# First phase of a gated attention and FFN kernel: x tiles and GELU results move on GpSimd's DMA queue instead of SP's

## The chip, the cores and the metric

The kernel runs on one core of one Trainium2 chip. The metric is the device time of one execution in microseconds, as the median over runs. The core has five instruction streams: PE (TensorE, matmuls), DVE (VectorE), ACT (ScalarE), POOL (GpSimd) and SP (SyncE, which here only issues DMAs). Each stream runs in order, and streams wait for each other through semaphores. SP and POOL both issue DMAs. Those of SP are counted as queue q1 in the profile, those of POOL as q0.

## What is computed

The input x has 2048 tokens of width 1024 in bfloat16. Two branches are mixed by a sigmoid gate `g` of `x . gate_w`:

```
for s in range(64):                      # segments of 32 tokens
    h = concat(mem, x[32*s : 32*s+32])   # 8 memory rows and 32 tokens
    q, k, v = h@Wq, h@Wk, h@Wv           # 32 heads of 128
    p = softmax(mask(q k^T / sqrt(128))) # the last mask is causal on 40 rows
    o = (p v) @ Wo
    mem, a[s] = o[:8], o[8:]             # the memory of the next segment
b   = (gelu(x @ w_gate) * (x @ w_up)) @ w_down   # width 3584
out = g * a + (1 - g) * b
```

The recurrence through `mem` makes the 64 segments sequential. The FFN branch `b` doesn't depend on it.

## The kernel before, in words

All instructions are recorded by one helper, `op` (line 79), as (engine, function, what it reads, what it writes). The recorder finds the dependencies between the operations and turns them into semaphore waits. The order on each engine is the order of recording. A DMA also names a `lane`, which is a semaphore of its own; a DMA waits for the one before it on the same lane to land.

**First phase** (lines 402 to 587, some 97 us). It prepares x, computes a part of the FFN and fills the on-chip weight slots.

- `load_x(T)` (472) loads tile T of 128 tokens (256 KB) into one of four buffers `px`. `do_x(T)` (476) transposes it on PE (L485), copies it on ACT into `xTp` (L489, L490) and its last columns on DVE into `xr` (L491). POOL multiplies it by `gate_w` into the single buffer `gp` (L493) and DVE reduces that into `dl` (L498). So a `px` buffer has two readers, PE and POOL.
- After four tiles, `xTp` and `xr` are stored to HBM as `xq_scr` (L500) and `xr_scr` (L503). There are two buffers of each.
- `pre_j(fb, j)` (451) computes one of the first four of 28 FFN feature blocks for one of four blocks of 512 tokens: two groups of eight matmuls (L446) and `gelu` (432: L434, L437 on ACT; L435, L438, L440 on DVE) into `gpre[fb % 2]`. When four are done, `gpre` is stored to HBM as `g_scr[fb]` (L458). The FFN loads it at the end of the kernel.
- `more` and `more_late` issue weight pieces (`fetch`, L370) of 512 KB into slots `sl`, three pieces a step.

The loop (566 to 583) walks 16 steps (fb, j). In each it records the next `do_x`, the loading of the tile four further on, three weight pieces, the stores that are due, and `pre_j`. All these DMAs are recorded on SP. The stores wait in two lists, `puts` and `slow`:

```python
now, puts[:], slow[:] = list(puts), slow, []
```

A store in `puts` is recorded in the next step. A store in `slow`, which is the one of `gpre`, passes into `puts` first and is recorded one step later.

**Recurrent loop** (lines 859 to 1006). A segment's 64 weight pieces are walked in an order called `ORDER` (k0, q0, v0, k1, q1, o0, v1, o1; 0 and 1 are halves of the heads). Projections are L758 and L770. The last 8 tokens of each segment, the tails, don't depend on the memory row by row, so their q, k and v are computed for four segments at a time (`fill`, L785) and pass through HBM: `qk_scr` (L831, all on one lane `fq`) and `v_scr` (L826). POOL issues these stores and loads them again, the value tails into `vB` by `load_v` (L522). In segment 0, the tails of the first groups are made and stored between the projections, and `load_v(0, ...)` is called once for each half of the heads: the first recorded at v0, step 4, together with `rest_k(0)`, the second at k1. `attend_tail` (L734) reads `vB`. Some weight slots are shared by two pieces, and the second is fetched when the first is used up, such as six of the `Wv` pieces in segment 0. Every segment ends with the copy of the new memory into `hT` (L994).

**Second FFN part** (lines 1050 to 1107): the other 24 feature blocks, the down projection (L1098) and the mix into `out`.

Of the kernel before, what the change touches and what calls it, by code (L numbers as in the profile page):

```python
# [30 lines left out]
class _Prog:  # L31
# [47 lines left out]
    def op(self, eng, fn, rd=(), wr=(), lane=None, after=()):  # L79
        o = _Op(eng, fn)  # L80
        if lane is not None:
            ln = self.lanes.get(lane)
            if ln is None:
                ln = self.lanes[lane] = [self.new_sem(f"{self.name}_{lane}"), 0, None]
            if ln[2] is not None:
                o.deps.append(ln[2])
            ln[1] += 16
            o.sem, o.val, o.inc, o.need = ln[0], ln[1], 16, True
            ln[2] = o
        for r in rd:  # L90
            self._touch(o, r, False, lane is not None)
        for r in wr:
            self._touch(o, r, True, lane is not None)
        o.deps.extend(after)
        if eng == "pool" and lane is None:
            if self.pool is not None:
                o.deps.append(self.pool)
            self.pool = o
        for d in o.deps:
            d.need = True  # L100
        o.idx = len(self.ops)
        self.ops.append(o)
        return o
# [92 lines left out]
def bass_gated_mix__memory_aug_recurrent_mem_tr__geglu_ffn__prompt_kernel(  # L196
# [15 lines left out]
    xf = A_x.flatten_outer_dims()  # L212
# [18 lines left out]
    with ExitStack() as es:  # L231
# [21 lines left out]
        g_scr = nc.dram_tensor("g_scr", [NFB, 128, NJP * FB], BF16)  # L253
# [91 lines left out]
        op = P.op  # L345
# [45 lines left out]
        for g in range(4):  # L391
            q = slice(32 * g, 32 * g + 32)
# [13 lines left out]
        NPX = min(NT, 4)  # L406
        px = [al(f"px{i}", [128, D]) for i in range(NPX)]
# [43 lines left out]
        def pre_j(fb, j):  # L451
            bg, bu = 2 * (j % 2), 2 * (j % 2) + 1
            for bk, w in ((bg, wgp), (bu, wup)):
                up(w[2 * j // NJP], xTp[fb % 2], bk, 128 * (j % (NJP // 2)))
            g = gpre[fb % 2]
            gelu(PB[bg][:, 0:FB], PB[bu][:, 0:FB], bg, bu, j, g[:, j, :], g.r(j * FB, (j + 1) * FB))
            if j == NJP - 1:
                slow.append(lambda: op("sp", lambda e: e.dma_start(g_scr[fb], g[:, :, :].rearrange("p j c -> p (j c)")), rd=[g.r()],  # L458
                                       wr=[("D", "g", fb)], lane=f"gw{fb % 2}"))

        puts, slow = [], []
# [7 lines left out]
                ins = e.transpose(PBV[5][:, kc * 8:(kc + 1) * 8], pm[0:8, kc * 128:(kc + 1) * 128], ident[0:8, 0:8])  # L469
            return ins  # L470

        def load_x(T):
            if T < NT:
                op("sp", lambda e: e.dma_start(px[T % NPX][:, :], xf[T * 128:(T + 1) * 128, :]), wr=[px[T % NPX].r()], lane=f"px{T % NPX}")

        def do_x(T):
            t = px[T % NPX]
# [43 lines left out]
        def load_v(s, us=slice(0, 2)):  # L521
            op("pool", lambda e: e.dma_start(vB[:, us, :].rearrange("p u c -> p (u c)"),  # L522
                                             v_scr[s][:, :, us, :].rearrange("i h u c -> h i (u c)")),
               rd=[("D", "v", s // 4, g, u) for g in range(4) for u in range(us.start, us.stop)], wr=[vB.r()], lane="vb")

        op("sp", lambda e: e.dma_start(pm[0:8, :], mem0[:, :]), wr=[pm.r()], lane="pm")
        load_x(0)
        op("act", lambda e: e.dma_start(gwb[:, :], gate_w.rearrange("(o d) -> o d", o=1).to_broadcast([128, D])),
           wr=[gwb.r()], lane="gw")
        for T in range(1, NPX):  # L530
            load_x(T)
        def load_pre(h):
            for w, W, nme in ((wgp[h], B_w_gate, "gp"), (wup[h], B_w_up, "up")):
                c0, c1 = h * NJP * 64, (h + 1) * NJP * 64
# [20 lines left out]
        for T in range(TB):  # L555
            do_x(T)
            load_x(T + NPX)
            if T == 0:
                op("dve", lambda e: e.tensor_copy(hT[:, :, NR:32], memT[:, :].rearrange("p (k c) -> p k c", k=KC)),
                   rd=[memT.r()], wr=[hT.r()])  # L560
                op("dve", lambda e: e.tensor_copy(hT[:, :, 0:NR], xTp[0][:, 0, 0, :, 0:NR]),
                   rd=[xTp[0].r(0, KC * SEG)], wr=[hT.r()])
# [3 lines left out]
        for fb in range(NFB):  # L566
            for j in range(NJP):
                T = TB * (fb + 1) + j
                now, puts[:], slow[:] = list(puts), slow, []
                if T < NT:  # L570
                    do_x(T)
                    load_x(T + NPX)
                if T == NT:
                    op("act", lambda e: e.activation(gal[:, :], dl[:, :], ACTF.Exp, scale=-1.0), rd=[dl.r()], wr=[gal.r()])
                    op("dve", lambda e: e.tensor_scalar(out=dl[:, :], in0=gal[:, :], scalar1=1.0, scalar2=None, op0=ALU.add),
                       rd=[gal.r()], wr=[dl.r()])
                    op("dve", lambda e: e.reciprocal(gal[:, :], dl[:, :]), rd=[dl.r()], wr=[gal.r()])
                more(3)
                if T >= NT:
                    more_late(2 if j < 3 and not inits else 0)  # L580
                for f in now:
                    f()
                pre_j(fb, j)
# [250 lines left out]
        def mm0(m, u, b, t, G=0, h=hR):  # L834
            for f in fill(m, u, b, h):
                f()
            act_copy(t[:, :], PB[b][:, :], [BK(b)], [t.r()])
            if m == "v":
                fill_store(m, u, G, t)

        def tr0(m, u, t, n, G=0):
            op("pe", lambda e: trans4(e, t), rd=[t.r(), ident.r()], wr=[BK(TT)])
            fill_put(st0[n], "dve")
            if G == 0:
                x = 256 * u + 128 * (m == "k")
                op("pool", lambda e: e.tensor_copy(qkr[:, u, 0 if m == "q" else 1, :], st0[n][:, 0:128]), rd=[st0[n].r(0, 128)],
                   wr=[qkr.r(x, x + 128)])
            fill_store(m, u, G, st0[n])

        def rest_k(r):  # L850
            op("pool", lambda e: e.tensor_copy(kT[:, :, :, 32:40].rearrange("p j g c -> p (j g) c"),
                                               qkr[:, r, 1, :].rearrange("p (x c) -> p x c", c=8)),
               rd=[qkr.r(256 * r + 128, 256 * r + 256)], wr=[kT.r()])
# [5 lines left out]
        for s in range(NSEG):  # L859
# [12 lines left out]
            def on(m, r, n, *fs):  # L872
                at.setdefault(base_of[m, r] + n, []).extend(fs)
# [10 lines left out]
            if s == 0:  # L884
                on("k", 0, 0, lambda: mm0("v", 0, F1, st0[3]))
                on("k", 0, 0, lambda: mm0("k", 0, F2, tokB))
                if NG > 1:
                    on("k", 0, 0, lambda: mm0("k", 0, F1, tok, 1, hR1))
                    on("k", 0, 4, lambda: tr0("k", 0, tok, 1, 1))
                on("k", 0, 0, lambda: tr0("k", 0, tokB, 0))  # L890
                on("q", 0, 0, lambda: mm0("q", 0, F1, tokB))
                if NG > 1:
                    def q_next():
                        for f in fill("q", 0, F2, hR1):
                            f()
                        tr0("q", 0, tokB, 2)
                        act_copy(tokB[:, :], PB[F2][:, :], [BK(F2)], [tokB.r()])
                    on("q", 0, 0, q_next)
                    on("q", 0, 3, lambda: tr0("q", 0, tokB, 3, 1))
                else:  # L900
                    on("q", 0, 3, lambda: tr0("q", 0, tokB, 2))
                on("v", 0, 4, lambda: (rest_k(0), load_v(0, slice(0, 1))))

                def fills_1():
                    mm0("k", 1, F1, tok)
                    for f in fill("q", 1, F2):
                        f()
                    tr0("k", 1, tok, 1)
                    act_copy(tok[:, :], PB[F2][:, :], [BK(F2)], [tok.r()])
                    mm0("v", 1, F1, st0[2])  # L910
                    tr0("q", 1, tok, 3)
                on("k", 1, 0, fills_1)
                if NG > 1:
                    on("k", 1, 0, lambda: op("dve", lambda e: e.tensor_copy(hR[:, :, :], hR1[:, :, :]), rd=[hR1.r()], wr=[hR.r()]))
                on("k", 1, 0, lambda: (load_v(0, slice(1, 2)), more_late(99)))
                on("q", 1, 0, lambda: load_h(1))
# [73 lines left out]
            if not last:  # L990
                for t, bk in enumerate((B1, B2)):
                    op("pe", lambda e, t=t, bk=bk: e.transpose(PBV[bk][:, 0:128], a_bf[:, 128 * t:128 * t + 128], ident[:, :]),
                       rd=[a_bf.r(128 * t, 128 * t + 128), ident.r()], wr=[BK(bk)])
# [3 lines left out]
                       rd=[BK(bk)], wr=[h_next.r(32 * kc, 32 * kc + 32) for kc in range(t, KC, 2)])  # L997
# [53 lines left out]
        for fb in range(NFB):  # L1051
# [20 lines left out]
            for ps in range(NPS):  # L1072
# [15 lines left out]
                for c in range(NWD):  # L1088
# [3 lines left out]
                    for jj in range(WD):  # L1092
                        j = c * WD + jj

                        def f(e, w=w, jj=jj, j=j, bank=bank, tbs=tbs):
                            for k, tb in enumerate(tbs):
                                for hf in range(2):
                                    ins = e.matmul(PB[bank[2 * k + hf]][:, :], lhsT=GT[:, j, tb * 128:(tb + 1) * 128],  # L1098
                                                   rhs=w[:, jj, hf * 512:(hf + 1) * 512], start=(j == 0), stop=(j == NJ - 1))
                            return ins  # L1100
# [43 lines left out]
```

## Time and profile before

| | us |
|---|---|
| median of 7 runs (lowest to highest) | 2233.7 (2230.86 to 2240.97) |
| the profiled execution's own time | 2235.38 |
| its span, first to last instruction | 2233.6 |
| PE busy | 2083.4 (93%) |
| DVE, ACT, POOL busy | 904.5, 610.7, 616.7 |
| DMA moved | 529.04 MB, mean 237 GB/s |
| first L785 (end of the first phase) | 97.07 |
| first `hT` copy of L994 (end of segment 0) | 151.8 |
| 62 segments from there, mean | 24.49 |

Times in the profile count from the first instruction of the span. A wait line reads "who waited, for whom: total us, times, longest". In the chain of waits each line is a start, a length and what the end of the kernel was waiting for at that time. A name such as `px<-in_A_x_dram` is a DMA by destination and source, with buffer numbers left out.

### The profile page before, as it was taken

The page shows a single profiled execution, that of the slowest core. Times are in us where ns is not written, and L with a number is a line of the kernel's source. Part 1 is how long each engine was busy: PE and PEld are TensorE (multiplying, and loading weights), DVE is VectorE, ACT ScalarE, POOL GpSimd, SP SyncE. Part 2 cuts the span into 40 slices and gives each one's busy share as a digit, 9 for nine tenths or more (in the row PEclk, how much of TensorE's full clock was granted, in tenths as well). Part 3 has the DMA queues.
Part 4 walks back from the last instruction along what each step waited for, and adds up shares of the span by engine and source line. Part 5 has one row for each costly group of instructions (what it writes and reads, how often), then busy time and mean ns, then how long its engine had stood idle before and what let it go on. Part 6 is the DMA issues. An engine that isn't in the chain of part 4 may idle for free.

```text
span 2233.6 us, 80061 instructions
## 1 busy us (share of the span) xinstructions
PE 2083.4 (93%) x36642; PEld 1097.9 (49%) x36642; DVE 904.5 (40%) x2152; ACT 610.7 (27%) x1296; POOL 616.7 (28%) x1139
## 2 busy tenths in 40 slices
PE   7888999999999999999999999999888999999999
PEld 3344555455555545555555545555454444444444
DVE  5433343334334333433433344334434616354362
ACT  4322232323223232323223232223222303122130
POOL 5123333332433343233333423343331000000000
PEclk9889999999999999999999999999999999999999
DMA  9977888788788888887888788778879410001000
GB/s 320 384 266 280 279 308 282 274 301 315 264 290 309 283 275 279 291 291 272 294 298 278 266 296 305 271 272 319 281 268 369 172 38 29 29 24 33 19 29 19
DMA packets 203440, 529.04 MB, mean 237 GB/s; under 512 B 29592, under 2 KB 46616, under 8 KB 203104
## 3 DMA queue, kind: packets, MB, share of 16 engines
q1 hardware_dynamic: 174064, 471.93, 59.2%
q0 software_dynamic: 28896, 51.75, 7.3%
q8 instruction: 287, 4.70, 0.8%
q10 hardware_dynamic: 144, 0.26, 0.1%
q14 instruction: 49, 0.40, 0.0%
HBM read 490.16 MB, written 33.55 MB: 234 GB/s over the span
## 4 chain that ended last, share of the span: by engine, by line
PE 75%; DMA 12%; POOL 5%; issue 4%; DVE 2%; ACT 1%; SPq 1%; DVEq 0%; POOLq 0%
PE pb L758 24%; PE pb L446 16%; PE pb L770 8%; PE pb L1098 8%; PE pb L785 7%; DMA sl<-in_A_Wo_dram 4%; PE pb L670 4%; PE pb L800 3%; DMA a_scr<-a_bf 2%; DMA sl<-in_A_Wv_dram 2%; PE pb L691 2%; DMA sl<-in_A_Wk_dram 1%; POOL v_scr L826 1%; PE pb L685 1%; PE pb L1080 1%
## 5 line engine op out<-in xcount | busy, mean ns | idle before, releaser
L758 PE MATMUL pb<-sl,hT 128*32 128x512 bf16 x12288 | 750.0, 382 | 21.1 <-issue 8.2
L758 PEld LDWEIGHTS pb<-sl,hT 128*32 128x32 bf16 x12288 | 330.8, 97 | 289.8 <-issue 20.5
L770 PE MATMUL pb<-sl,oT 128*32 128x256 bf16 x8192 | 283.5, 277 | 47.7 <-issue 39.9
L658 ACT ACTIVATE tok<-pb 128x512 bf16<-128x512 f32 x317 | 189.3, 597 | 402.1 <-PE pb L758 366.7
L743 POOL COPY oRc<-oT 128x128 bf16<-128x128 bf16 x128 | 97.2, 760 | 639.9 <-DVE oT L661 620.7
L770 PEld LDWEIGHTS pb<-sl,oT 128*32 128x32 bf16 x8192 | 209.7, 97 | 97.9 <-issue 51.2
L785 PE MATMUL pb<-sl,hR 128*32 128x512 bf16 x3072 | 225.5, 384 | 5.9 <-DMA sl<-in_A_Wv_dram 4.9
L446 PE MATMUL pb<-xT,wg 128*128 128x512 bf16 x768 | 183.1, 382 | 4.1 <-DMA wg<-in_B_w_gate_dram 4.1
L446 PE MATMUL pb<-xT,wu 128*128 128x512 bf16 x768 | 181.7, 379 | 0.0
L1098 PE MATMUL pb<-wd,GT 128*128 128x512 bf16 x784 | 169.9, 379 | 0.0
L661 DVE CAST oT<-pb 128x160 bf16<-128x160 f32 x256 | 71.0, 319 | 211.4 <-PE pb L734 211.3
L658 ACT ACTIVATE vA<-pb 128x512 bf16<-128x512 f32 x128 | 76.4, 597 | 266.7 <-PE pb L758 266.7
L434 ACT ACTIVATE s<-pb 128x512 f32<-128x512 f32 x112 | 66.9, 597 | 293.7 <-PE pb L446 293.7
L661 DVE COPY kT<-pb 128x512 bf16<-128x512 bf16 x128 | 51.9, 406 | 229.4 <-PE pb L670 90.3
L670 PE MATMUL pb<-ident,tok 128*128 128x128 bf16 x1268 | 126.7, 222 | 6.2 <-DVE kT L661 2.4
L670 PEld LDWEIGHTS pb<-ident,tok 128*128 128x128 bf16 x1268 | 72.3, 98 | 115.1 <-ACT tok L658 86.4
L435 DVE SCALAR_TENSOR_TENSOR tp<-s,pb 128x512 f32<-128x512 f32 x112 | 76.7, 684 | 127.2 <-ACT s L434 126.8
L446 PEld LDWEIGHTS pb<-xT,wg 128*128 128x128 bf16 x768 | 75.3, 98 | 95.8 <-issue 6.4
L1098 PEld LDWEIGHTS pb<-wd,GT 128*128 128x128 bf16 x784 | 76.7, 98 | 92.5
L696 DVE TENSOR_REDUCE st<-pb 128x8 f32<-128x320 f32 x128 | 62.9, 491 | 143.6 <-PE pb L691 143.6
L446 PEld LDWEIGHTS pb<-xT,wu 128*128 128x128 bf16 x768 | 75.3, 98 | 91.2 <-issue 1.0
L1045 POOL DMA_DIRECT2D out_dram<-osb x14 | 7.6, 545 | 372.5 <-PE pb L446 224.6
(96 smaller groups left out, 2148.5 us busy)
## 6 DMA issues: line engine op xcount, KB each, us to landing
sl<-in_A_Wv_dram SPq DMA_DIRECT2D x394, 512.0 KB, 8.8
sl<-in_A_Wo_dram SPq DMA_DIRECT2D x205, 512.0 KB, 6.0
sl<-in_A_Wk_dram SPq DMA_DIRECT2D x142, 512.0 KB, 5.5
sl<-in_A_Wq_dram SPq DMA_DIRECT2D x79, 512.0 KB, 7.1
qkr<-qk_scr POOLq DMA_DIRECT2D x126, 64.0 KB, 2.2
qk_scr<-stg POOLq DMA_DIRECT2D x61, 128.0 KB, 5.9
wd<-in_B_w_down_dram SPq DMA_DIRECT2D x7, 1024.0 KB, 15.2
px<-in_A_x_dram SPq DMA_DIRECT2D x16, 256.0 KB, 6.8
```

What stands on the lines that cost most here:

```text
L434: op("act", lambda e: e.activation(s1[:, :], hg, ACTF.Square, scale=SQ), rd=[BK(bg)], wr=[s1.r()])
L435: op("dve", lambda e: e.scalar_tensor_tensor(out=t[:, :], in0=s1[:, :], scalar=1.0, in1=hg, op0=ALU.add, op1=ALU.mult), rd=[BK(bg), s1.r() ...
L446: ins = e.matmul(PB[bk][:, 0:FB], lhsT=w[:, kc, cc:cc + 128], rhs=x[:, :, :, kc, :].rearrange("p t i c -> p (t i) c"), start=(kc == 0), st ...
L658: op("act", lambda e: e.activation(o, i, ACTF.Copy), rd=rd, wr=wr)
L661: op("dve", lambda e: e.tensor_copy(o, i), rd=rd, wr=wr)
L670: ins = e.transpose(PBV[TT][:, j * 128:(j + 1) * 128], t[:, j * 128:(j + 1) * 128], ident[:, :])
L743: op("pool", lambda e: e.tensor_copy(oRc[:, u, :, :].rearrange("p c x -> p x c"), oT[:, :, :, 32:40].rearrange("p g j c -> p (g j) c")), r ...
L758: ins = e.matmul(PB[bk][32 * g:32 * g + 32, :], lhsT=h[:, i, :], rhs=w[:, g * 512:(g + 1) * 512], start=(p % 8 == 0), stop=(p % 8 == 7))
L770: ins = e.matmul(PB[XO][32 * g:32 * g + 32, 0:256], lhsT=oT[:, gp_, 2 * jj + hh, 0:32], rhs=w[:, c:c + 256], start=(r == 0 and p % 8 == 0 ...
L785: ins = e.matmul(PB[b][32 * g:32 * g + 32, :], lhsT=h[:, k[2], :], rhs=w[:, g * 512:(g + 1) * 512], start=(n == 0), stop=(n == 7))
L800: ins = e.matmul(PB[b][32 * g:32 * g + 32, 0:256], lhsT=t[:, :, 2 * i + hh], rhs=w[:, c:c + 256], start=(ends[0] and i == 0 and hh == 0), ...
L1098: ins = e.matmul(PB[bank[2 * k + hf]][:, :], lhsT=GT[:, j, tb * 128:(tb + 1) * 128], rhs=w[:, jj, hf * 512:(hf + 1) * 512], start=(j == 0) ...
```

## The change

Three things are moved, and nothing is computed differently.

- `load_x` gets an engine argument. The first four tiles still load from SP; the other twelve are issued by POOL, each behind the POOL product of the tile whose buffer it takes.
- The store of `gpre` into `g_scr` is issued by POOL. It is recorded in the step after its last `gpre`, behind that step's `do_x` and ahead of its x load; it no longer passes through `puts`.
- In segment 0 the first `load_v` is recorded at q0 instead of v0, step 4. On POOL it moves from behind the fourth `qk_scr` store to ahead of the third.

On SP's stream the weight pieces and the `xq_scr` and `xr_scr` stores remain in the first phase, in the same order. PE's, ACT's and DVE's instructions stay in the same order.

```diff
             if j == NJP - 1:
-                slow.append(lambda: op("sp", lambda e: e.dma_start(g_scr[fb], g[:, :, :].rearrange("p j c -> p (j c)")), rd=[g.r()],
+                slow.append(lambda: op("pool", lambda e: e.dma_start(g_scr[fb], g[:, :, :].rearrange("p j c -> p (j c)")), rd=[g.r()],
                                        wr=[("D", "g", fb)], lane=f"gw{fb % 2}"))
...
-        def load_x(T):
+        def load_x(T, eng="pool"):
             if T < NT:
-                op("sp", lambda e: e.dma_start(px[T % NPX][:, :], xf[T * 128:(T + 1) * 128, :]), wr=[px[T % NPX].r()], lane=f"px{T % NPX}")
+                op(eng, lambda e: e.dma_start(px[T % NPX][:, :], xf[T * 128:(T + 1) * 128, :]), wr=[px[T % NPX].r()], lane=f"px{eng}{T % NPX}")
...
-        load_x(0)
+        load_x(0, "sp")
...
         for T in range(1, NPX):
-            load_x(T)
+            load_x(T, "sp")
...
                 T = TB * (fb + 1) + j
-                now, puts[:], slow[:] = list(puts), slow, []
+                now, puts[:] = list(puts), []
                 if T < NT:
                     do_x(T)
-                    load_x(T + NPX)
+                for f in slow:
+                    f()
+                del slow[:]
+                load_x(T + NPX)
...
                 on("k", 0, 0, lambda: tr0("k", 0, tokB, 0))
+                on("q", 0, 0, lambda: load_v(0, slice(0, 1)))
                 on("q", 0, 0, lambda: mm0("q", 0, F1, tokB))
...
-                on("v", 0, 4, lambda: (rest_k(0), load_v(0, slice(0, 1))))
+                on("v", 0, 4, lambda: rest_k(0))
```

## The prediction

> **What bounds the kernel now.** I first cut the start of the execution into its stages (first phase 0 to 97 us, then the recurrent loop) with the table by stretches; columns are busy time of each engine, granted clock, DMA share, GB/s.
>
> ```profile
> 13.00:43.00 30.00, 26.21 (x144) 12.76 (x144) 20.23 (x32) 13.42 (x24) 17.03 (x8) 1.00 0.96 333
> 43.00:97.00 54.00, 43.38 (x208) 19.56 (x208) 29.59 (x46) 17.99 (x34) 12.78 (x6) 0.87 1.04 405
> 97.00:152.00 55.00, 45.10 (x797) 21.01 (x796) 13.17 (x35) 12.58 (x26) 16.90 (x32) 0.88 0.76 265
> 152.00:222.00 70.00, 63.27 (x1434) 33.36 (x1438) 27.86 (x78) 19.92 (x45) 21.73 (x45) 1.00 0.82 296
> ```
>
> From 43 to 97 us the DMA engines are full (1.04, 405 GB/s) while PE is busy only 43.4 of 54 us at clock 0.87. From 152 us the loop runs, at 23 to 27 us a segment, with DMA not full: a segment that starts earlier ends earlier, so what is won ahead of 152 us should be kept. Next the waits in 30 to 100 us, and those of the SP queue in 0 to 200 us (total, times, longest):
>
> ```profile
> DVE gpre L440 <- DMA g_scr<-gpre: 8.3, 2, 6.4
> ACT xTp L489 <- DMA xq_scr<-xTp: 5.5, 1, 5.5
> ...
> PE pb L485 <- DMA px<-in_A_x_dram: 5.2, 3, 3.6
> ...
> POOL gp L493 <- DMA px<-in_A_x_dram: 2.4, 1, 2.4
> ```
>
> ```profile
> SPq L474 <- POOL gp L493: 16.8, 8, 4.0
> SPq L458 <- DVE gpre L440: 5.5, 1, 5.5
> ```
>
> Three transfers hold compute: x tiles (`px`), the store of transposed x (`xq_scr`), the store of GELU results (`g_scr`). In return SP, which issues in order, stands behind GpSimd's products before it may reload an x tile. The tile view of `px` from 30 to 80 us says how long an x tile takes:
>
> ```profile
> DMA to landing us min/median/max: 9.9/12.0/13.8
> ```
>
> That is a queue of weight pieces ahead of it, as pieces land every 1.25 to 1.3 us. Last, the chain of waits from 42 to 140 us:
>
> ```profile
> 54.93 10.02 DMA g_scr<-gpre
> ...
> 75.96 10.50 DMA g_scr<-gpre
> 86.55 0.70 DVE gpre L440
> 87.30 9.84 PE pb L446 x32
> 97.14 5.29 PE pb L785 x96
> ...
> 103.52 6.34 DMA qk_scr<-stg
> ...
> 110.39 2.71 DMA qk_scr<-stg
> ...
> 113.51 8.14 DMA qk_scr<-st
> ...
> 122.49 6.12 DMA qk_scr<-st
> ...
> 130.20 5.54 DMA v_scr<-st
> ...
> 136.48 1.97 DMA vB<-v_scr
> ```
>
> Two `g_scr` stores set the end of the first phase. After it a row of `qk_scr` stores on GpSimd's queue (one lane, each waits for the last) leads to the second value-tail load, which frees the attention at 138.6.
>
> **What the Trainium skill says.** "DMA: Bandwidth & Descriptors", Issuing engines are not separate DMA queues: SP's and GpSimd's transfers share 16 engines. So no bandwidth is gained. The same page, Queues, rings and completion order: each engine takes turns between queue rows, packet by packet, so a transfer on GpSimd's row need not stand behind SP's backlog. The trace agrees: GpSimd's 128 KB stores land in 6.0 to 8.1 us while SP's 512 KB pieces take 9 to 14. "SBUF — State Buffer", Who interferes with whom: a Vector instruction with at most one SBUF input and in no 2-port mode does not block GpSimd. Vector's phase-one operations read PSUM or reduce one SBUF tile; no run here shows the case. "TensorE: Matmul & The Clock Gate", The HAM clock gate: an idle window of about 3.4 us halves PE's clock. The trace fits: the step after the 5.8 us gap at 81 to 87 us took 6.2 us where a full one takes 3.45.
>
> **The change, part by part.**
>
> *Pace of the first phase.* A step is one feature block for 512 tokens (two L446 groups), the first twelve with an x tile each. Undisturbed, `gpre` starts are 25.67, 29.70, 33.72, 37.75, 41.77: 4.03 us a step, set by Vector (0.28 + 1.21 + 0.68 + 0.69 + 0.69) and its 0.70 wait for ACT's tanh. Steps without an x tile need 3.45 us (starts 70.99 and 74.44). Step 5 starts its matmuls at 38.55. With no DMA wait step 12 starts at 38.55 + 7 x 4.03 = 66.8 and the phase ends at 66.8 + 4 x 3.45 = 80.6, not 97.1: **16.5 us earlier**. That is the ceiling.
>
> *x tiles on GpSimd.* Twelve loads leave SP and its 16.8 us of waits go. An x tile is issued right after its predecessor's product, and used four steps, 16 us, later, some 14 us after issue. Its landing isn't in the trace for this size on this queue: from below 2.9 us (the 256 KB `asb` loads, queue free), from above 12 us (it stands in the backlog after all). I take 7 us, the 128 KB stores plus half a tile. Anything under 14 costs nothing.
>
> *GELU stores on GpSimd.* Four leave SP, and go one step sooner, since `slow` no longer passes through `puts`. The first is issued at 38.5 (its last `gpre` ends 38.44) instead of 54.93, and is needed at 54; the second near 55, needed near 69, instead of 75.96 with a need at 80.1. Landing: from below 4.7 us (the fastest `g_scr`), from above 10.5 (the slowest); either is in time. Both `g_scr` waits, 8.3 us, and the cold clock behind them go.
>
> *What GpSimd issues.* 12 x 0.56 (the `hT` and `vB` rows) + 4 x 0.56 to 0.78 = 9 to 10 us, in its 1.9 us of idle time a step. The tightest place: product 8 ends 37.95, the store waits for `gpre` until 38.44, store and tile take until 39.6 (40.1 at 0.78 each), the next product started at 39.84 and its reader at 42.58, 0.6 us after it ended. Behind that waiting store stand only the x load and that product: 0, at most 0.2 us.
>
> *SP's queue.* Without the x waits it issues weight pieces from 5 us on. DMA moved 196 GB/s from 10 to 20 us and 322 from 20 to 30; filled, that is nearly 3 MB, or 7 us of DMA, brought forward. `xq_scr` of tokens 512 to 1023 stays on SP's queue: ready at 34, behind 4 MB that share with x tiles, it lands at 51 to 55, and ACT wants its buffer at 53. Cost 0 to 2 us, taken as 1.
>
> *After the phase.* What is late next is DMA. The six `Wv` pieces that are refetched into shared slots last landed at 124.85, with 43.5 MB moved by then (sum of the 10 us stretches). Filled from the start: 6.2 MB by 20 us, the other 37.3 MB at 405 GB/s, 92 us, gives 112; and 3 us for the short rows of `qk_scr` (294 GB/s at share 0.885 from 100 to 120) gives **115**. PE now asks for them at 101 instead of 117.5, so its stall there grows from 7 to 14 us. The lane of `qk_scr` stores starts 6.4 us after the phase, at 87; all four now meet a full DMA, so 6.5 + 6.5 + 8 + 6.1 us and 1.4 between them: 115. Both meet there, against 128.7 before (when Vector got on): 13 us. With the 1 us of `xq_scr`: **12 us**. Bounds: 16.5 (ceiling) and 7, if the idle DMA share ahead of 125 us (2.4 + 3.5 + 0.7 + 1.5 + 1.6, less 2.4 of start) is all there is to win.
>
> *Value tails.* The first `vB` load moves ahead of the third `qk_scr` store. Attention waits for the second load (landed 138.45), not the first (128.9), and there GpSimd waits for the lane anyway (2.06 and 4.58 us against 0.56 of issue): nothing, bounds +0.6 and -0.6.
>
> The profiled execution took 2235.4 (span 2233.6), 1.7 over the median 2233.7. Less 12: 2223.4 for it, 2221.7 for the median; I say 2222.
>
> **The rivals.**
> 1. *DMA is the whole bound*: pieces come as fast as they can, only 5 to 7 us of idle DMA are won: 2227 to 2229. For: share 1.04 over 54 us. Against: three named waits of compute in that stretch, on transfers that are not weights.
> 2. *The stall moves to `xq_scr`*: GpSimd's queue takes half the engines, SP's store lands at 58 as before, the phase ends at 85.6, the lane at 120: 8.5 us, 2225. For: the store stays on the full queue. Against: its backlog starts 7 us sooner.
> 3. *GpSimd's queue starves*: slower. With four buffers a step cannot be shorter than (landing + 3) / 4. It decides at 18.6 us of landing: then a step takes 5.4, tile 15 starts at 79 and the phase ends at 97. At 24 us it would end at 112: 2248. Against: the longest landing seen on that queue in this stretch is 8.1 us.
> 4. *It doesn't act*: if loads were held by the tile's other reader (PE), nothing is sooner: 2234. Against: PE's transposes start within 1 us of the product in every step.
>
> **How the numbers follow.** Likeliest case 0.76 (7 to 16.5 us), rivals 2 and 1 together 0.14, rival 4 0.04, rival 3 0.06. A difference of under 0.2%, 4.5 us, can't be told from none; faster is under 2229.2. Faster takes the first case, rival 2 and half of rival 1: 0.85; same 0.08; slower 0.07. The likeliest case gives 2217 to 2227; the ends with 2 us of spread of a median, the ceiling and rival 1 give 2214 to 2230.
>
> **What would show it.** Right: GpSimd's x tiles land in under 14 us; no wait of `gpre` on `g_scr`; L785 starts at 80 to 83; GB/s near 390 from 10 to 30 us; the last refetched `Wv` at 113 to 117; first `hT` copy of L994 at 139 to 142 instead of 151.8; segment times unchanged. Wrong: ACT waits on `xq_scr` over 3 us, products waiting on `px`, or segments longer by more than 0.2 us on average.

## The result, and the profile after

The changed kernel took **2221.36 us** (median of 12 runs, 2215.92 to 2229.59), the kernel before 2235.43 (median of 31). The ratio is 0.9936, interval 0.9923 to 0.9949: 14 us sooner, and 11 to 17 with the interval. Forecast were 2222 and 12 us. The profiled execution has a span of 2220.1 us, 13.5 less than before.

The change adds lines, so L785 of before is now L788, L734 is L737, L826 and L831 are L829 and L834, and L994 is L998. Where the prediction put a mark, these times stand (us from the start of the span):

| mark | before | predicted | after |
|---|---|---|---|
| first L788, end of the first phase | 97.1 | 80 to 83 | 83.0 |
| last refetched `Wv` piece lands | 124.9 | 113 to 117 | 113.4 |
| Vector gets on behind lane and `Wv` | 128.7 | 115 | 115.0 |
| second `vB` load lands | 138.5 | - | 125.9 |
| first `hT` copy | 151.8 | 139 to 142 | 138.6 |
| mean of the 62 segments behind it | 24.49 | unchanged | 24.47 |

The table by stretches of the changed kernel, with the columns of the one shown before (us, the busy time of PE, weight loads, DVE, ACT, POOL, then clock, DMA share, GB/s):

```profile
13.00:43.00 30.00, 27.24 (x157) 13.69 (x156) 20.23 (x32) 14.51 (x26) 22.52 (x18) 1.00 1.04 405
43.00:97.00 54.00, 51.44 (x439) 23.98 (x441) 32.94 (x53) 21.66 (x40) 19.20 (x18) 1.00 1.04 406
97.00:152.00 55.00, 43.20 (x846) 20.35 (x842) 15.67 (x45) 12.59 (x27) 17.23 (x34) 0.88 0.79 292
152.00:222.00 70.00, 63.77 (x1407) 33.25 (x1398) 27.12 (x76) 19.65 (x45) 22.68 (x45) 1.00 0.80 284
```

Two things changed. From 13 to 43 us DMA moves 405 GB/s where it moved 333. From 43 to 97 us DMA was full before and is just as full now, yet PE is busy 51.4 us instead of 43.4, at clock 1.00 instead of 0.87: a full DMA was not what held PE there. The waits of the changed kernel from 30 to 100 us (total, times, longest) show what is left:

```profile
POOL g_scr L458 <- DVE gpre L440: 12.2, 2, 11.4
POOL gp L493 <- DVE dl L498: 11.2, 8, 2.3
...
POOL px L474 <- POOL gp L493: 1.5, 5, 0.3
...
ACT xTp L489 <- DMA xq_scr<-xTp: 1.3, 1, 1.3
```

No row is left in which anybody waits for `g_scr` or for an x tile. GpSimd, which now issues both, stands ahead of a `g_scr` store for `gpre`, but the 11.4 us come when it has no more products to make. The tile view of `px` from 30 to 80 us:

```profile
DMA to landing us min/median/max: 5.9/6.1/7.7
```

Before it was 9.9/12.0/13.8, on the same 16 DMA engines with as much to do. The four `g_scr` stores were issued at 38.81, 54.91, 73.09 and 85.12 and landed 7.0 to 7.9 us later. Last, the chain of waits of the changed kernel (start, length, what was waited for):

```profile
34.04 20.33 DMA xq_scr<-xTp
...
72.53 10.53 PE pb L446 x48
83.07 5.29 PE pb L788 x96
...
89.52 6.36 DMA qk_scr<-stg
...
96.68 5.66 DMA qk_scr<-stg
...
102.82 5.76 DMA qk_scr<-st
...
109.38 5.54 DMA qk_scr<-st
...
117.60 3.65 issue
...
123.96 1.90 DMA vB<-v_scr
...
138.63 0.18 DVE hT L998
```

The `g_scr` pieces have gone from it. The one transfer left in the first phase is `xq_scr`, which the change left on SP. The last three steps of the phase run as one piece of 10.53 us, at full clock. Behind the phase the lane of `qk_scr` stores is unchanged in kind and only starts sooner.

### The profile page after: what moved, and what is told of

It reads as the page before. It is cut to its first block, busy times and chain, and to the rows that moved or that the text cites. A ratio compares the mean times of both kernels' runs of the same rounds, so it can differ in the third digit from the quotient of the medians.

```text
span 2220.1 us, 80064 instructions
## 1 busy us (share of the span) xinstructions
PE 2076.6 (94%) x36642; PEld 1097.1 (49%) x36642; DVE 906.4 (41%) x2152; ACT 610.4 (27%) x1296; POOL 625.9 (28%) x1155
## 4 chain that ended last, share of the span: by engine, by line
PE 79%; DMA 10%; POOL 4%; issue 4%; DVE 2%; ACT 1%; SPq 0%; POOLq 0%; DVEq 0%; ACTq 0%
PE pb L761 26%; PE pb L446 16%; PE pb L773 9%; PE pb L1102 8%; PE pb L788 7%; PE pb L673 4%; PE pb L803 3%; DMA sl<-in_A_Wo_dram 3%; DMA a_scr<-a_bf 2%; PE pb L694 2%; DMA sl<-in_A_Wv_dram 1%; PE pb L688 1%; POOL v_scr L829 1%; PE pb L727 1%; PE pb L1084 1%
## 5 line engine op out<-in xcount | busy, mean ns | idle before, releaser
L788 PE MATMUL pb<-sl,hR 128*32 128x512 bf16 x3072 | 227.0, 385 | 8.1 <-DMA sl<-in_A_Wv_dram 3.5
```

Of the source, the lines that this page charges most:

```text
L788: ins = e.matmul(PB[b][32 * g:32 * g + 32, :], lhsT=h[:, k[2], :], rhs=w[:, g * 512:(g + 1) * 512], start=(n == 0), stop=(n == 7))
```

## The experiments

All ratios are to the kernel before, with 95% intervals; 0.001 is 2.2 us. The marks (phase end, `Wv`, first `hT`) are from one profiled execution each. They are more exact than its total, since the loop behind them varies by some us from execution to execution, but they vary too: the changed kernel, the one without the `vB` move and the one with the lane opened (below) have the same first phase, and it ended at 83.0, 83.1 and 82.0. So a difference of one microsecond between two marks shows no effect.

### The three parts, one by one

The change has three parts. Each was put alone into the kernel before, and the third was also taken out of the changed kernel.

**Only the x tiles on GpSimd** (the diff's `load_x` lines, nothing else):

```diff
-        def load_x(T):
+        def load_x(T, eng="pool"):
...
```

> Only the twelve x tiles move to GpSimd's queue; the GELU stores stay on SP and one step late, vB as before. Theory (each named wait holds compute by itself): x waits and the SP waits on POOL go, early DMA fill as in the full change, but the first g_scr store is issued near 50 us behind a full queue, lands near 62 and is needed at 54 to 55: gpre waits about 7 us, and 2 to 3 us at the second; first phase ends near 93 (97 before, 83 with the full change); total 4 to 6 us under before. Rival (DMA is the whole bound, the gain is the early fill alone): nearly the whole gain, 11 to 14 us under before.

Measured: 0.9958 (0.9942 to 0.9974), some 9 us. The phase ended at 89.5, `Wv` landed at 117.4, first `hT` 143.9. The gain lies between the two expectations (4 to 6 us, and 11 to 14). `xq_scr` was waited for 0.2 us, x tiles landed in 5.8 to 7.3 us, and in its waits from 30 to 100 us only the other stall is left:

```profile
DVE gpre L440 <- DMA g_scr<-gpre: 7.0, 2, 5.1
```

That is less than the 9 to 10 us expected of it. Two things change together with the x tiles: they land in half the time, and SP, which no longer waits for GpSimd's products, issues weight pieces sooner (363 GB/s from 10 to 20 us instead of 196). No run here separates the two.

**Only the `g_scr` stores on GpSimd, one step sooner** (the `slow` lines of the diff, nothing else):

```diff
-                slow.append(lambda: op("sp", ...
+                slow.append(lambda: op("pool", ...
...
-                now, puts[:], slow[:] = list(puts), slow, []
+                now, puts[:] = list(puts), []
...
+                for f in slow:
+                    f()
+                del slow[:]
```

> Only the GELU stores move to GpSimd's queue and one step sooner; x tiles stay on SP, vB as before. Theory: the second gpre wait (6.4 us) and the cold clock behind it go, x tiles still land after 12 us and pace steps 7 to 11; first phase ends at 87 to 89; the shared Wv pieces land near 121; total 7 to 9 us under before. Rival (DMA is the whole bound): no early fill, so 0 to 2 us under before.

Measured: 0.9964 (0.9951 to 0.9978), 8 us; phase end 90.9, later than the 87 to 89 expected; first `hT` 145.1. DMA still moved only 191 GB/s from 10 to 20 us. So a gain comes without the early filling of DMA: bandwidth was not the whole bound, and the waits of compute counted. Those that stay are on x tiles (7.2 us of PE), `xq_scr` (6.8) and `xr_scr` (7.8). At the phase end the two parts add up: 7.6 us sooner with the x tiles alone and 6.2 with the stores alone, against 14.1 with both.

**Only the `vB` move**, in the kernel before and taken out of the changed one:

```diff
+                on("q", 0, 0, lambda: load_v(0, slice(0, 1)))
...
-                on("v", 0, 4, lambda: (rest_k(0), load_v(0, slice(0, 1))))
+                on("v", 0, 4, lambda: rest_k(0))
```

> Before, with the first value-tail load alone moved ahead of the third qk_scr store. Theory: no difference (under 1 us), since attention waits for the second load. Rival (that load held the chain): 1 to 3 us faster.

> The full change without the value-tail move. Theory: as the full change, 13 to 14 us under before. Rival: 1 to 3 us of the gain lost.

Measured: 1.0003 (0.9989 to 1.0016) with it alone, and 0.9930 (0.9906 to 0.9955) for the change without it, where the second `vB` load landed at 125.5 against 125.9. The third part does nothing for the time.

### What the `g_scr` stores gain: the queue or the sooner issue

The change does both at once, so each was tried with the stores on SP at the new, sooner place: in the changed kernel, and in the kernel before with x tiles still on SP.

```diff
-                slow.append(lambda: op("pool", lambda e: e.dma_start(g_scr[fb], ...
+                slow.append(lambda: op("sp", lambda e: e.dma_start(g_scr[fb], ...
```

> The full change, but the GELU stores are issued by SP at the same early place (ahead of the step's three weight pieces) instead of by GpSimd. Theory (what counts is that the store is issued a step early and that SP no longer waits on POOL; the queue itself is secondary): SP stands until gpre is ready at 38.4 and 54.6, stores land 12 to 14 us later, 51 to 53 and near 67, still ahead of the need at 55 and 72; xq_scr lands 2 to 3 us later, so the phase ends near 85; total 10 to 12 us under before. Rival (the store must not stand behind weight pieces): gpre waits 5 us or more, total 5 to 7 us under before.

> Kernel before with one thing changed: the g_scr stores stay on SP, but are recorded one step sooner (behind that step's do_x, no longer passing through puts). x tiles stay on SP, the vB load where it was. Theory (the sooner issue is what the stores gain, not the queue): the first is issued near 39, lands near 50 and is in time for gpre at 54; no or under 1 us of wait of gpre on g_scr; the phase ends at 90 to 93 as with the stores on GpSimd at that place (90.9), total -6 to -9 us against before, ratio 0.996 to 0.9975. Rival (the queue is what they gain while x tiles hold SP): SP stands in its waits for products, the stores are issued late or land late, gpre still waits 3 us or more, phase end 94 to 98, total 0 to -4.

Measured: 0.9938 (0.9918 to 0.9959) in the changed kernel, 14 us where 10 to 12 were expected, with the phase end at 83.4. In the kernel before: 0.9970 (0.9957 to 0.9983), 7 us, with the phase end at 89.3, against 90.9 with the stores on GpSimd.

The second of these runs also tells which of the two waits on `g_scr` counted. Its first store was issued at 38.44 and landed at 52.68, but `gpre` wrote that buffer again only at 64.12, against 65.04 before. Until then the chain of waits goes through another store:

```profile
42.82 16.67 DMA xq_scr<-xTp
```

So the first wait of before was mostly hidden behind `xq_scr`. The second store was issued at 60.84 instead of 75.96 and landed at 74.86, and the `gpre` that had waited for it starts at 80.03 instead of 86.55. That is the gain. The waits of this kernel from 30 to 100 us have no `g_scr` any more; what DMA still holds is

```profile
ACT xTp L489 <- DMA xq_scr<-xTp: 6.5, 1, 6.5
...
POOL gp L493 <- DMA px<-in_A_x_dram: 3.3, 1, 3.3
...
PE pb L485 <- DMA px<-in_A_x_dram: 2.8, 2, 2.3
```

So for these stores the queue is worth nothing that can be measured; the 15 to 16 us by which they are issued sooner are the gain.

### What meets at 113 to 115 us

The prediction had two things end together there: the `Wv` pieces and the `qk_scr` lane. First the `Wv` pieces were helped, by fetching six `Wo` pieces behind them instead of ahead:

```diff
-                    more_late(2 if j < 3 and not inits else 0)
+                    more_late(2 if j < 1 and not inits else 0)
...
-        more_late(8 - len(hosts) + spare + len(late))
+        more_late(0)
```

> The full change, with the six Wo pieces of the end of the first phase issued behind the six shared Wv pieces of segment 0 instead of ahead of them: 3.1 MB, 8 us of DMA, less ahead of Wv. Theory (DMA bytes and the qk_scr lane meet at the same time, 113 to 115): the shared Wv land near 105 instead of 113.4, but the lane still frees its buffer at 114.9, so the total is as the full change, within 1.5 us of 14 under before. Rival (the bytes alone bind): 6 to 8 us more, 20 to 22 under before.

Then the lane was opened, so that a `qk_scr` store doesn't wait for the one before it:

```diff
-                   rd=[st.r()], wr=[("D", "qk", G, m4)], lane="fq")
+                   rd=[st.r()], wr=[("D", "qk", G, m4)], lane=f"fq{m4}{G % 2}")
```

> The full change, with the qk_scr stores on separate lanes by kind and group parity instead of one, so that none waits for the last one's landing. Theory: the four stores land by 105 or so instead of 114.9, then the shared Wv (113.4) alone holds; Vector gets on about 1 us sooner and the later stores need no lane, so the value tails come 1 to 3 us sooner: 15 to 17 us under before. Rival (the lane alone binds): 6 to 9 us more, 20 to 23 under before.

And both together:

> Both of the last two edits on top of the full change. Theory: with neither the bytes ahead of Wv nor the lane, Vector gets on at 106 to 108 instead of 115; less what late Wo pieces cost, 18 to 23 us under before, clearly more than the sum of the two single effects. Rival (something else holds at 115, or the loop takes it back): 13 to 16 under before.

| | ratio (interval) | phase end | last `Wv` | Vector gets on | first `hT` |
|---|---|---|---|---|---|
| changed kernel | 0.9936 (0.9923 to 0.9949) | 83.0 | 113.4 | 115.0 | 138.6 |
| `Wo` behind | 0.9960 (0.9948 to 0.9973) | 82.2 | 110.2 | 113.4 | 142.7 |
| lane open | 0.9951 (0.9935 to 0.9967) | 82.0 | 113.5 | 114.8 | 138.1 |
| both | 0.9949 (0.9935 to 0.9964) | 84.1 | 112.5 | 113.7 | 139.2 |

None gained in total. With the lane open, its four stores had landed by 101.7, but the chain of waits goes through the weight pieces instead, and Vector gets on at the same time:

```profile
99.09 14.43 DMA sl<-in_A_Wv_dram
...
116.24 5.64 DMA v_scr<-st
...
122.66 2.07 DMA vB<-v_scr
```

With `Wo` behind, the chain stays on the lane, whose fourth store now lands at 113.33, and no more than 1.6 us is won. Counted from the end of each kernel's own phase, Vector gets on 32.0, 31.2, 32.7 and 29.6 us later: either edit alone is worth less than 1 us there, both together 2.4 (all other profiles of this text lie between 31.1 and 32.7). So two limits do lie side by side. In the kernel with both, the 2.4 us are lost again, as its second `vB` load takes 5.0 us instead of 1.9. The 105 us that I expected of `Wv` failed, and so did 18 to 23 us for both together. A refetched piece can only be issued when PE has used up what lay in its slot, at 97.0 to 99.6 in the kernel with `Wo` behind; its six pieces then took 13.2 us from the first issue to the last landing, against 15.6 in the changed kernel (97.8 to 113.4) and 13.0 before. Six pieces of backlog were worth 2.4 us, not 8.

The kernel with `Wo` behind even lost some 5 us of the gain. Its chain of waits at the end:

```profile
114.92 5.88 DMA v_scr<-st
...
121.10 4.06 issue
125.17 4.03 DMA vB<-v_scr
```

The last `vB` load takes 4.03 us instead of 1.90; the moved `Wo` pieces were landing until 129. Ahead of it GpSimd stands 4.06 us for the landing of a `v_scr` store that it had issued late itself, in a pause that is taken up at the end of this text. Together they put the `vB` landing at 129.2 instead of 125.9, and PE, which waits for it, 3.3 us back.

### GpSimd's room, and its four buffers

The stores that still stand on SP were moved to GpSimd as well:

```diff
-                puts.append(lambda: op("sp", ... xq_scr ...
+                puts.append(lambda: op("pool", ... xq_scr ...
-                puts.append(lambda: op("sp", ... xr_scr ...
+                puts.append(lambda: op("pool", ... xr_scr ...
```

> Changed kernel with the xq_scr and xr_scr stores issued by GpSimd too. Theory (prediction's step on xq_scr: the second store waits behind SP's backlog of pieces, and that is all it costs): ACT's 1.3 us wait on xq_scr goes, the first phase ends at 81 to 82 instead of 83.0, and because the shared Wv pieces and the qk_scr lane meet again at 113 to 115, the total moves by 0 to -1.5 us against the changed kernel: ratio to the kernel before 0.992 to 0.994. Rival (GpSimd's queue has no room left: 0.8 MB more on it delays x tiles that are issued behind the stores): x tiles land in over 10 us, PE or products wait on px, phase ends at 84 or later, total +1 to +5.

Measured: 0.9949 (0.9934 to 0.9963), not distinguishable from the change. ACT's wait on `xq_scr` was gone, as expected, but the phase ended at 83.5 and not at 81 to 82. The rival's mechanism doesn't fit either: x tiles landed in up to 12.2 us, but PE waited for them only 0.9 us. What took the gain is GpSimd's own time. An `xq_scr` store takes 0.77 us to issue, and where the two stores are issued, the next product starts late: 4.52 us behind the last instead of 3.45 (20.36 to 24.88), and 5.67 instead of 4.03 (36.41 to 42.08). Steps of `gpre` in those places took 4.54, 5.12 and 4.67 us instead of 4.03. That is 2.2 us lost, where the changed kernel lost 1.75 to `xq_scr` (one step of 5.78). With the lane open, whose first phase is the same, that step took 4.72, so the 1.75 is itself uncertain by a microsecond. A row of the waits of this kernel, which the changed kernel doesn't have, is the trace of it:

```profile
DVE dl L498 <- POOL gp L493: 1.6, 2, 1.0
```

The same with the lane open:

> Changed kernel with both: xq_scr and xr_scr stores on GpSimd, and each qk_scr store on its own lane. Theory (the last shared Wv piece, issued only when PE has used up its slot, holds Vector once the lane is free): the phase ends near 81.5, PE uses the slots up to 1.5 us sooner, Wv lands at 112 to 113.5 and Vector gets on at 113 to 114.5: 0 to -2 us against the changed kernel, ratio 0.992 to 0.9935. Rival (DMA bytes alone set Wv's landing): no change against the changed kernel, Wv at 113.4 and Vector at 115.

Measured: 0.9953 (0.9938 to 0.9969), `Wv` at 113.8, Vector on at 115.1. As the phase didn't end sooner (83.7), this doesn't tell its two theories apart; it shows no version faster than the changed kernel.

Last, x tiles with two of the four buffers:

```diff
-        NPX = min(NT, 4)
-        px = [al(f"px{i}", [128, D]) for i in range(NPX)]
+        NPX = min(NT, 2)
+        px = [al(f"px{i}", [128, D]) for i in range(4)]
```

> Changed kernel with x tiles using two of the four px buffers (the memory stays allocated; tiles 2 and 3 are then loaded by GpSimd behind products 0 and 1). Theory of the prediction's rival 3, tried at another size: a step with an x tile cannot be shorter than (landing + 3) / buffers; at the measured 6.1 us and two buffers that is 4.55 us instead of 4.03, so over the some 12 steps the phase ends 5 to 7 us later, at 88 to 90, with PE and GpSimd waiting on px; the total is 3 to 7 us over the changed kernel, ratio 0.994 to 0.997. If the landing shrinks with fewer tiles in flight (4 to 5 us), the step stays at 4.03 and nothing changes: phase end 83 to 84. If the landing grows with SP's backlog to 9 us, the step is 6 us and the phase ends at 100 or later, slower than before.

Measured: 1.0003 (0.9985 to 1.0020), the whole gain gone. Tiles landed in 5.5 to 9.0 us, median 6.2, but now compute waits for them (waits from 30 to 100 us):

```profile
POOL gp L493 <- DMA px<-in_A_x_dram: 10.3, 5, 4.7
PEld pb L485 <- DMA px<-in_A_x_dram: 9.0, 5, 4.1
...
PE pb L485 <- DMA px<-in_A_x_dram: 6.8, 4, 3.6
```

The products 2 to 15 start at 14.98 to 77.21, 4.79 us apart on average, where (6.2 + 3) / 2 says 4.6. The phase ended at 95.4 instead of 83.0, 12.4 us later; I had expected 5 to 7, with 12 tiles instead of 14 and the shorter step. The first `hT` copy came at 151.2, 12.6 later, and the median is 14 us over that of the changed kernel: what is lost ahead of the loop is kept through it, as what is won is.

## Why the prediction was right, point by point

- **Pace and ceiling.** The steps of 4.03 us run undisturbed to the eighth `gpre` at 53.93. One step, of 5.78, waits for `xq_scr`; then it is 4.03 again. 80.6 and 1.75 make 82.4. The other 0.6 us are a wait that no step of mine held: the first of the last four steps starts at 68.60, as worked out, but PE then outruns Vector, waits for `gpre` until 72.5, and takes 3.93 us for it instead of 3.45. The parts that the prediction adds up for Vector's step come to 4.25 us; the 4.03 is the measured distance of the `gpre` starts, and nothing else rests on the parts.
- **`xq_scr` on SP.** Expected to land at 51 to 55 and to cost 0 to 2, taken as 1. It landed at 54.37 and cost 1.75. Rival 2 had it at 58 and fails.
- **x tiles.** 7 us was taken, 6.1 measured, and under 14 it indeed cost nothing. The prediction's reading of the Trainium skill, "DMA: Bandwidth & Descriptors", Queues, rings and completion order, agrees with this case: with SP's queue full, a tile on GpSimd's queue lands in 6.1 us (median), and took 12.0 in SP's. The stores that it quoted from the trace of before were weaker support: one of 128 KB, at 110.39, had landed in 2.7 us, outside its 6.0 to 8.1, and DMA wasn't full there. Rival 3, that this queue starves, fails with four buffers; with two buffers its mechanism is there, and takes the whole gain. Rival 4, that PE holds the loads, fails: the tile load at 34.29, for one, is issued 0.3 us after its predecessor's product.
- **GELU stores.** In time, as worked out. But the prediction made no difference between the queue and the sooner place, and the experiments show that the place did it. It also counted both waits, 8.3 us; in the kernel before, the first was mostly hidden behind `xq_scr`.
- **GpSimd's issues.** Costed at 0 to 0.2, hidden in 1.9 us of idle time a step. The products of the tight place start at 39.95 and 43.95, against 39.84 and 43.86 before: 0.1. With the `xq_scr` and `xr_scr` stores added, the same idle time was too short.
- **Filling DMA.** Expected near 390 GB/s from 10 to 30 us; measured 366 from 10 to 20 and 402 from 20 to 30. By 113.4 us 43.9 MB have moved, which agrees with the 43.5 of the ledger. Rival 1, that only 5 to 7 us of idle DMA can be won, fails: `Wv` landed 11.4 us sooner. Its count of idle DMA share was too low a measure of the bytes that were lost: before, a share of 0.69 from 10 to 20 us moved 196 GB/s, and after, 1.10 moves 366, more bytes for the same share.
- **Behind the phase.** 115 was right for Vector, but that it came out to the tenth is luck, for several terms were off. The lane started at 89.5 and not at 87, which was counted from the ceiling, and then ran 25.4 us instead of 28.5: every store took 5.5 to 6.4 us, and none 8. The errors nearly cancel. For `Wv`, the bytes moved since the start were named as the cause of 115. But in all fourteen profiles the first of the six pieces is issued 14.8 us behind the end of the phase, when PE has used up its slot, however much DMA has moved by then; the backlog ahead of it is worth the 2.4 us that `Wo` behind showed. So what lies behind the phase moves with it: Vector gets on 31.6 us behind it before, 32.0 with the change, and 32.5 with the `g_scr` stores alone, which hardly fill DMA early. PE was said to come to these pieces at 101 instead of 117.5, with a stall growing from 7 to 14 us. It came to them at 107.7, after a 2.0 us stall for a `Wk` piece at 101, and its weight loads waited 5.0 us for `Wv`, less than the 6.7 of before. That step was wrong without harm, because Vector waits for the last piece and not for PE's first.
- **Value tails.** Nothing, as said.
- **The sum.** 12 forecast, 14 measured; the interval, 11 to 17, holds both. In the profile 14.1 us at the phase end become 13.7 at Vector and 13.2 at the first `hT` copy, and the segments are unchanged. The 1 us taken off for `xq_scr` didn't arise at Vector, because the shorter `qk_scr` stores made up for the later start.

## What to carry to other kernels

A store that waits a step in a list behind a full queue can hold a buffer longer than its bandwidth would: look first at when it is issued, and only then at which queue it takes. A small transfer that is needed soon can gain from another queue than the one with the long backlog of weights, as long as the engine that issues it has idle time ahead of its own work; count every issue against that idle time. Before helping one transfer, look for the next limit: here two ended within 2 us of each other, and taking away either gave nothing. And look at what the stretch behind is tied to: here it starts from the end of the phase, so that time won there is kept.

## What was not expected of the hardware

- With the first `vB` load moved ahead, GpSimd pauses 3.2 to 4.1 us between its third and fourth `v_scr` store of segment 0, waiting for nothing that the profile names ("117.60 3.65 issue" in the chain above). This is so in all six profiles of kernels with that move and a single `qk_scr` lane, and each time the fourth store is issued 0.34 us after the `qk_scr` store four issues ahead has landed. In the five without the move the fourth store goes out at once, while that `qk_scr` store is still under way. The three with the move and an open lane don't pause, but there that store had landed before. That looks like a limit on what GpSimd may have outstanding, though a mere count of DMAs doesn't fit the five. The kernel sets `nc.dynamic_dma_scratch_size` to 2048 (line 260), and no run changed that: the cause stays open. The pause is mostly hidden in the changed kernel (the second `vB` load lands 0.3 us later than without the move) and lies on the chain in the one with `Wo` behind.
- A 1 MB `xq_scr` store took 12.7 to 20.3 us from issue to landing on SP's queue in the changed kernel, and 11.5 to 13.4 on GpSimd's.
